# Retention attention and a gated feed-forward layer on one core: batches 0 and 1 held two positions a partition, the first stage reordered, and two groups of block 0 computed by halves of tokens

## The chip, the core and the metric

The kernel runs on one core of one Trainium2 chip. The core has five engines that each work through their own list of instructions in order and wait for each other by semaphores: TensorE (PE in the profile, its weight loads PEld), VectorE (DVE), ScalarE (ACT), GpSimd (POOL) and SyncE (SP), which here issues nearly all DMAs. Matmul results land in PSUM, which here is handed out in tiles with tags (`mm` three, `O` two, `sc` two, `st` one); GpSimd works on SBUF alone in this kernel. The metric is the device time of one execution in microseconds (us), less is better. Before: 293.27 us, the median of three runs (292.98 to 293.93).

## The reference, cut to what matters

```python
batch, n_heads, seq, head_dim = (8, 8, 576, 64)
scores = scale * np.matmul(q, k.transpose(0, 1, 3, 2))
gamma = 1.0 - 2.0 ** (-5.0 - np.arange(H))
Dmat = np.where(rel >= 0, gamma[:, None, None] ** rel[None, :, :], 0.0)   # rel = i - j
ret = scores * Dmat[None, :, :, :]
attn_out = np.matmul(ret, v)
x = attn_out.transpose(0, 2, 1, 3).reshape(B * S, H * D)      # 4608 x 512
h = x @ w_in                                                  # 512 x 2048
g = h * (1.0 / (1.0 + np.exp(-beta * h)))
out = g @ w_out                                               # 2048 x 512
```

The decay gamma^(i-j) splits into a factor of the query and one of the key's value, so `q` is multiplied by gamma^i and `v` by gamma^-j once, and the masked product needs only zeros and ones.

## The kernel before, in words

**Blocks.** The first 512 positions of each batch are one block of tokens for the feed-forward part; the last 64 positions of all eight batches form block 8. A block's feed-forward has two halves: `up` (`ph`, 16 groups of 128 columns of `w_in`, four matmuls of 512 tokens each, then Silu on ScalarE into `gT`) and `down` (`po`, or from block 3 on the seven products of `seven_mm`, chains U, W and Z). Attention of later batches is woven into the feed-forward of earlier blocks.

**Attention of batches 0 and 1.** A batch's 512 positions are four chunks of 128, one position a partition. For each chunk: `pre` casts keys to `kn` and scales values to `vn` on GpSimd; `t_k` turns `kn` on TensorE into `T`, copied to `kT`; `a_sc` makes the chunk's scores `sc`, 8 matmuls with 64 rows and 128 columns, and DVE masks them into `R`; `a_O` adds up `vn` times `R` in `O`; `a_cross` adds what comes from earlier chunks, queries times the state `sbd`; `a_st` adds the chunk to the state `st` (4 matmuls), copied to `sbd` in two halves; `a_x` copies `O` to `xT`, the transposed input of `up`. Queries are scaled by `pre_q` into `qs` (four instructions) and turned by `t_q` into `qT` in two halves of heads.

**Later batches** have their own forms (`scores`, `outputs4`, `crosses4`, `four_states`) in 64x64 tiles, four of which can be at work in four quadrants of the array; `paired` interleaves two lists of such matmuls. Their keys and queries are turned by DMA transposes on SP (`x_q`, `x_k`, line 372 in the profile).

**What sets the order.** The schedule is written out by hand. The first stage is the list of calls at the end (lines 869 to 915): each call puts its instructions into the queues of its engines, in that order. After it, `merged` walks through a list `fill` of TensorE pieces and puts the steps of several `streams` before the piece whose number they name: `d0` is the number of block 0's first down, `u1` of block 1's first up. `load_kv` and `load_q` put DMAs into SP's queue in the same way. Buffers are reused in turn (keys and values `kvn`: 6, queries `qn`: 2, `qs`: 1, `qT`: 2, `kn` and `kT`: 4, `vn`: 7, `R`: 3), and an instruction that fills one waits for the last reader of it.

**SP's queue at the start**: queries of batch 0 in two halves of heads, then keys and values chunk by chunk as `ahead` says, then `w_in` in eleven pieces and `w_out` in eight, then queries, keys and values of batch 1, and so on. Keys and values move as rows of 64 floats, 256 bytes each; queries of four positions as rows of 1,024 bytes; weights of 1,024 and 2,048 bytes.

**Warm-ups** (`warm_up`) are matmuls on zeros that stand before waits in the first stage.

## Time and profile before

| what | value |
|---|---|
| median of three runs | 293.27 us |
| profiled execution, time | 292.41 us |
| its span (first to last instruction) | 290.7 us |
| mean granted TensorE clock | 0.999 |
| TensorE busy | 281.9 us, 97% |
| VectorE, ScalarE, GpSimd busy | 186.1, 171.5, 139.1 us |
| first matmul of the first `up` starts | 18.44 us |
| first `down` of block 0 starts | 32.34 us |
| batch 1's attention on TensorE | 42.7 to 56.0 us |

The table of stretches gives the time by stage: 0 to 18.4 us is batch 0's attention, where TensorE is busy in most of each microsecond with small matmuls and warm-ups; from there to 32 us block 0's `up`; to 50 us its `down`, with batch 1's attention in its last third and in the first part of block 1's `up`; then two blocks with plain downs and, from 111 us on, the blocks with seven products; the last matmul of the last block ends at about 287 us, and the last stores end the span.

How to read the profile: a row names the line of the program, the engine, the operation, what is written from what, the shape and the number of instructions; in rows in order of time the first two numbers are start and length in us, and the brackets say how long the engine stood idle before and who ended that wait. A busy TensorE is not one at its peak, since matmuls overlap; 512 columns follow each other every 0.216 us in the `up` here, though one shows 379 ns. The profiled run is one execution, and its time lies 0.86 us under the median.

### The profile page before, as it was taken

Reading aid. Unit: us, or ns where it says so; the run is one execution under the profiler, and the core shown is the slowest. Engines: PE = TensorE matmul, PEld = TensorE weight load, DVE = VectorE, ACT = ScalarE, POOL = GpSimd, SP = SyncE. Lnnn points to the kernel's source line nnn. Section 1 sums busy time; section 2 is a strip of 40 time slices with the busy share of each in tenths; the row PEclk is TensorE's granted clock in tenths of the full one; section 3 lists DMA queues with packets and bytes.
Section 4 is the critical chain, followed back from the end, with each engine's and each line's share of the span. In section 5 each row is a group of like instructions: output and inputs, shape, how many; then the busy total and the mean of one; then the engine's idle time right before and its main releaser. Section 6 shows DMA issues by size and latency. Waiting matters only on the chain.

```text
span 290.7 us, 8297 instructions
## 1 busy us (share of the span) xinstructions
PE 281.9 (97%) x3433; PEld 175.7 (60%) x3433; DVE 186.1 (64%) x340; ACT 171.5 (59%) x301; POOL 139.1 (48%) x259
## 2 busy tenths in 40 slices
PE   8799999999999998999999999999999999999995
PEld 6554446864544554448854885578547845784584
DVE  6563555804896396279889875995597555642673
ACT  5677546686878872765158625772576156837730
POOL 4766207872499397089759539625088100000000
PEclk9999999999999999999999999999999999999999
DMA  8999999996989999988999989990779430003004
GB/s 213 218 342 386 387 283 233 240 190 123 247 180 246 253 187 201 267 225 214 183 249 265 195 231 260 189 156 2 215 176 142 92 144 3 2 28 119 0 4 143
DMA packets 128886, 54.03 MB, mean 186 GB/s; under 512 B 110400, under 2 KB 121680, under 8 KB 128848
## 3 DMA queue, kind: packets, MB, share of 16 engines
q1 hardware_dynamic: 128816, 53.49, 77.9%
q8 instruction: 27, 0.44, 0.7%
q14 instruction: 11, 0.09, 0.1%
q10 hardware_dynamic: 32, 0.01, 0.0%
HBM read 36.71 MB, written 9.44 MB: 159 GB/s over the span
## 4 chain that ended last, share of the span: by engine, by line
PE 55%; DVE 5%; POOL 4%; DMA 2%; issue 1%; ACT 0%; SPq 0%; DVEq 0%
PE ph L727 27%; PE U L764 10%; PE Z L764 7%; PE W L764 6%; DMA qn<-in_q_dram 2%; DVE sa L748 2%; PE O L509 2%; PE po L837 2%; POOL vn L305 2%; POOL kn L364 1%; PE sc L509 1%; POOL qs L323 1%; PE st L509 1%; DVE gT L732 1%; DVE R L286 1%
## 5 line engine op out<-in xcount | busy, mean ns | idle before, releaser
L727 PE MATMUL ph<-xT,w_in_sb 128*128 128x512 bf16 (+1 forms) x560 | 116.8, 364 | 0.0
L727 PEld LDWEIGHTS <-w_in_sb 128*128 128x128 bf16 x560 | 53.3, 98 | 55.2 <-POOL w_in_sb L206 0.7
L734 ACT ACTIVATE gT<-ph,beta_sb 128x512 bf16<-128x512 f32 (+1 forms) x92 | 58.4, 642 | 42.6 <-PE ph L727 41.8
L764 PEld LDWEIGHTS <-sa 128*128 128x128 bf16 x480 | 46.9, 98 | 5.8 <-issue 0.2
L732 DVE TENSOR_SCALAR gT<-hs,ratio 128x512 bf16<-128x512 f32 x48 | 25.8, 538 | 32.9 <-ACT hs L731 32.6
L364 POOL CAST kn<-kvn 128x128 bf16<-128x128 f32 (+2 forms) x80 | 35.8, 483 | 22.3 <-DMA kvn<-in_k_dram 21.8
L323 POOL TENSOR_TENSOR qs<-qn,gq 128x256 bf16<-128x256 f32 x48 | 30.5, 667 | 33.2 <-DMA qn<-in_q_dram 23.4
L748 DVE TENSOR_TENSOR sa<-gT 128x1024 bf16<-128x1024 bf16 (+1 forms) x54 | 43.9, 854 | 1.4 <-PE Z L764 1.2
L731 ACT ACTIVATE hs<-ph,beta_sb 128x512 f32<-128x512 f32 x48 | 33.0, 688 | 19.0 <-PE ph L727 18.7
L837 PE MATMUL po<-w_out_sb,gT 128*128 128x512 bf16 x192 | 43.5, 379 | 0.0
L305 POOL TENSOR_TENSOR vn<-kvn,gv 128x256 bf16<-128x256 f32 x48 | 34.3, 739 | 1.2 <-DMA kvn<-in_v_dram 0.7
L837 PEld LDWEIGHTS <-gT 128*128 128x128 bf16 x192 | 18.1, 98 | 20.6
L764 PE MATMUL U<-b,sa 128*128 128x256 bf16 x192 | 22.9, 272 | 0.1
L764 PE MATMUL Z<-b,sa 128*128 128x256 bf16 x192 | 22.9, 273 | 0.0
L286 DVE TENSOR_TENSOR R<-sc,late 128x512 bf16<-128x512 f32 x24 | 15.4, 681 | 11.4 <-issue 10.2
L764 PEld LDWEIGHTS <-gT 128*128 128x128 bf16 x192 | 18.7, 98 | 3.5
L248 DVE TENSOR_TENSOR b<-wt 128x512 bf16<-128x512 f32 x20 | 16.4, 880 | 1.9 <-ACT wt L231 1.8
L417 DVE TENSOR_TENSOR R<-sc,causal 128x512 bf16<-128x512 f32 x16 | 10.2, 686 | 4.6 <-PE sc L413 4.5
L819 PE MATMUL ph<-xT,w_in_sb 128*128 128x512 bf16 x56 | 12.4, 379 | 0.2 <-ACT xT L470 0.2
L642 ACT CAST xT<-O 128x512 bf16<-128x512 f32 x19 | 9.8, 599 | 3.5 <-PE O L509 3.5
L764 PE MATMUL W<-b,gT 128*128 128x256 bf16 x96 | 11.5, 273 | 0.0
L764 PE MATMUL U<-b,gT 128*128 128x256 bf16 x96 | 11.5, 273 | 0.0
(118 smaller groups left out, 304.8 us busy)
## 6 DMA issues: line engine op xcount, KB each, us to landing
qn<-in_q_dram SPq DMA_DIRECT2D x16, 512.0 KB, 5.8
out_dram<-ot SPq DMA_DIRECT2D x32, 256.0 KB, 3.3
kvn<-in_k_dram SPq DMA_DIRECT2D x20, 256.0 KB, 5.4
kvn<-in_v_dram SPq DMA_DIRECT2D x20, 256.0 KB, 5.1
wt<-in_moe_w_out_dram SPq DMA_DIRECT2D x8, 512.0 KB, 9.3
kvn<-in_k_dram SPq DMA_DIRECT2D x24, 128.0 KB, 4.0
kvn<-in_v_dram SPq DMA_DIRECT2D x24, 128.0 KB, 3.4
wt<-in_moe_w_in_dram SPq DMA_DIRECT2D x5, 512.0 KB, 8.2
```

What stands on the lines that cost most here:

```text
L248: nc.vector.tensor_tensor(to, x, y, op)
L286: return lambda: f(*a)
L305: nc.gpsimd.tensor_tensor(vn[:, hs], v[:, hs], g[:, hs], ALU.mult)
L323: nc.gpsimd.tensor_tensor(batch[b]["qs"][:, cs, to], q_tiles[b][:, hs, cs].rearrange("p h i d -> p i h d"), gq[:, cs, hs].unsqueeze(3).to_ ...
L364: nc.gpsimd.tensor_copy(kn[:, c % 2, to], t[:, 0, hs])
L727: nc.tensor.matmul(ph, w_in_sb[:, ko, fo * P:(fo + 1) * P], xts[m][:, ko, :, w], start=(ko == 0), stop=(ko == KO - 1))
L731: nc.scalar.activation(h, ph, ACT.Silu, scale=beta_sb[:, fo:fo + 1])
L732: nc.vector.tensor_scalar(gts[m][:, fo], h, ratio[:, fo // 2:fo // 2 + 1], None, ALU.mult)
L734: nc.scalar.activation(gts[m][:, fo, :, w], ph, ACT.Silu, scale=beta_sb[:, fo:fo + 1])
L748: nc.vector.tensor_tensor(sums_a[0][:, held_in[j], ks], quarter(m, *x, ks), quarter(m, *y, ks), op)
L764: nc.tensor.matmul(chains[c, n][:, 0 if alone else p], a, sevens[k // 2][:, j - 1, k % 2, :], start=j in (3, 4, 1) and k == 0 and (alone o ...
L837: nc.tensor.matmul(po[:, :nn], gT[:, fo, ms, :], w_out_sb[:, fo, n0:n0 + nn], start=(fo == 0), stop=(fo == FO - 1))
```

## The change

- **Loads.** Keys and values of batches 0 and 1 come in spans of 256 positions (`load_span`), two neighbouring positions a partition, so that a row is 128 floats, 512 bytes; a span's keys are one DMA of 512 KB and its values another. In SP's queue keys of the first span go before the second half of the queries.
- **Tiles.** A chunk of 128 positions is now 64 partitions times two. `pre_k` and `pre_v` take each second position (r = 0, 1); scores (`a_sc`) and outputs (`a_O`) are 64x64 tiles with 128 columns, 16 to a call, a call covering a span and half the heads (y = 0, 1); `states` is 16 matmuls of 64x64 and 64 columns for one chunk, and for the first chunk of a batch also the same with all 128 partitions, which gives the state after two chunks; `state_out` copies it. `R` is masked by a mask of 256 columns.
- **Engines.** Of batch 0, one of the four `qs` goes to GpSimd, the first `qT` copy to DVE and the second to ScalarE in two parts, one `kn` to DVE, the `beta` copy to DVE; `w_in`'s first piece is cast by GpSimd alone. Chunk 2's `O` is split in two tiles like chunk 3's.
- **Order.** The first stage is a new list. `up_spans` computes groups 0 and 1 of block 0's `up` for tokens of chunks 0 and 1 inside it, and for chunks 2 and 3 as the first piece of `fill`. In batch 1, the transpose of the second half of a span's keys moves from `d0 + 14` to `d0 + 13.4` and the scores of the first call, which need both halves, stay at `d0 + 14`; the states of chunks 0 and 1 are both at `d0 + 15`.

Cut to its core, the diff is:

```diff
...
-    ahead = [(0, 0), (0, 1), (1, 0), (1, 1), (2, 0), (3, 0), (2, 1), (3, 1)]
-    keys_first = [(0, 0), (1, 0), (0, 1), (1, 1), (2, 0), (3, 0), (2, 1), (3, 1)]
+    def load_span(b, u, j):
+
+        t = stage.tile([P, H, 2, D], F32, name="kvn", tag="kvn", bufs=NQ)
+        nc.sync.dma_start(t[:].rearrange("p h r d -> p h (r d)"),
+                          (k, v)[j][b][:, 2 * u * P:2 * (u + 1) * P].rearrange("h (p r) d -> p h (r d)", r=2))
+        span_tiles[b, u, j] = t
...
-    load_q(0)
-    for n, j in ahead:
-        load_kv(n, (j,))
+    load_q(0, (0,))
+    load_span(0, 0, 0)
+    load_q(0, (1,))
+    load_span(0, 0, 1)
+    load_span(0, 1, 0)
+    load_span(0, 1, 1)
...
-    causal = consts.tile([P, P], BF16, name="causal")
+    causal = consts.tile([P, 2, CB, PC], BF16, name="causal")
     nc.gpsimd.memset(causal[:], 1.0)
-    nc.gpsimd.affine_select(out=causal[:], in_=causal[:], pattern=[[1, CB], [CB, PC]], compare_op=ALU.is_ge,
-                            fill=0.0, base=0, channel_multiplier=-1)
+    for x in range(2):
+        w = slice(x * TL, (x + 1) * TL)
+        nc.gpsimd.affine_select(out=causal[w], in_=causal[w], pattern=[[-1, 2], [1, CB], [CB, PC]], compare_op=ALU.is_ge,
+                                fill=0.0, base=0, channel_multiplier=-2)
...
-    def cast_w_in(g, kos=None):
+    def cast_w_in(g, kos=None, alone=False):
         t = wts[g]
         f0, fn, rows = pieces[g]
         for ko in kos or range(rows[0].start, rows[-1].stop):
-            if ko % 2 == 0:
+            if ko % 2 == 0 or alone:
                 nc.gpsimd.tensor_copy(w_in_sb[:, ko, f0:f0 + fn], t[:, ko])
...
-        nc.scalar.copy(beta_sb[:], pb[:])
+        nc.vector.tensor_copy(beta_sb[:], pb[:])
...
-            e = nc.vector
+            e = nc.gpsimd if b == 0 and n == 3 else nc.vector
...
+    def pre_k(b, u, r, copy=nc.gpsimd.tensor_copy):
+
+        if (b, u) not in spans:
+            spans[b, u] = dict(kn=sb.tile([P, 2, H, D], BF16, name="kn", tag="kn", bufs=4),
+                               kT=sb.tile([P, 2, HP, P], BF16, name="kT", tag="kT", bufs=4), vn=[None] * 2, R=[None] * 2)
+            live.update({b * CB + 2 * u + x: {} for x in range(2)})
+        copy(spans[b, u]["kn"][:, r], span_tiles[b, u, 0][:, :, r])
+
+    def pre_v(b, u, r):
+
+        vn = spans[b, u]["vn"][r] = sb.tile([P, H, D], BF16, name="vn", tag="vn", bufs=7)
+        nc.gpsimd.tensor_tensor(vn[:], span_tiles[b, u, 1][:, :, r], gains(gv, 2 * u + r), ALU.mult)
...
+    def t_q(b, u, rows=(slice(0, CB),)):
+        for cs in rows:
+            T = psum.tile([P, cs.stop - cs.start, 2, P], BF16, name="T", tag="mm" if u else "O", bufs=3 if u else 2)
+            for i in range(cs.start, cs.stop):
+                for p in range(2):
+                    nc.tensor.transpose(T[:, i - cs.start, p, :], heads(batch[b]["qs"][:, i], 2 * u + p), ident[:])
+            (nc.vector.tensor_copy if u == b else nc.scalar.copy)(batch[b]["qT"][:, cs, 2 * u:2 * u + 2], T[:])
+
+    def t_k(b, u, r):
+        late_span = b and u
+        T = psum.tile([P, HP, P], BF16, name="T", tag="sc" if late_span else "O" if b or u + r == 0 else "mm",
+                      bufs=2 if b or u + r == 0 else 3)
         for p in range(HP):
-            nc.tensor.transpose(T[:, p, :], heads(live[i]["kn"], p), ident[:])
-        (nc.vector.tensor_copy if i in (CB + 2, CB + 3) else nc.scalar.copy)(live[i]["kT"], T[:])
+            nc.tensor.transpose(T[:, p, :], heads(spans[b, u]["kn"][:, r], p), ident[:])
+        (nc.vector.tensor_copy if late_span or u > r else nc.scalar.copy)(spans[b, u]["kT"][:, r], T[:])
...
+    def a_sc(b, u, y):
+        L = spans[b, u]
+        L["R"][y] = R = sb.tile([P, 2, 2, 2, P], BF16, name="R", tag="R", bufs=3)
+
+        tag = ("O" if b else "mm") if y else "sc"
+        sc = [psum.tile([P, 2, 2, P], F32, name="sc", tag=tag, bufs=3 if tag == "mm" else 2) for _ in range(2)]
+
+        def one(j, r, pp, x):
+            rhs, view = q_cols(b * CB + 2 * u + x, row_d(j), 2 * y + pp)
+            mm(view(sc[j][half(x), r, pp, :]), L["kT"][row_d(j), r, 2 * y + pp, half(x)], rhs, start=True)
+
+        paired(*[[F(one, j, r, pp, x ^ j) for r in range(2) for pp in range(2) for x in range(2)] for j in range(2)])
+        m_b = causal[:].rearrange("k r i s -> k r (i s)").unsqueeze(2).to_broadcast([P, 2, 2, P])
         for j in range(2):
             nc.vector.tensor_tensor(R[:, j], sc[j][:], m_b, ALU.mult)
...
-        return i in (CB - 1, CB + 1)
+        return i in (CB - 2, CB - 1, CB + 1)
...
+    def a_O(b, u, y, crossed=(), last=True):
+
+        L = spans[b, u]
+
+        def one(x, pp, r, hh):
+            i, p = b * CB + 2 * u + x, 2 * y + pp
+            mm(O_of(i, p)[row_d(hh)], L["vn"][r][half(x), 2 * p + hh, :], L["R"][y][half(x), hh, r, pp, :],
+               start=opens(i, p) and r == 0 and x not in crossed, stop=last and r == 1)
+
+        paired(*[[F(one, x, pp, r, hh ^ x) for pp in range(2) for r in range(2) for hh in range(2)] for x in range(2)])
...
-            nc.vector.tensor_copy(x[:, :2], view(Os[0]))
-            nc.scalar.copy(x[:, 2:], view(Os[1]))
+            (nc.vector.tensor_copy if b else nc.scalar.copy)(x[:, :2], view(Os[0]))
+            (nc.scalar.copy if b else nc.vector.tensor_copy)(x[:, 2:], view(Os[1]))
...
+    def states(b, c):
+
...
+            state_ps[b] = psum.tile([P, 2, HP, D], F32, name="st", tag="st", bufs=1)
+        st, L = state_ps[b], spans[b, c // 2]
+        for n, rows in ((0, half(0)), (1, slice(0, P))) if c == 0 else ((1, half(c % 2)),):
+            for r in range(2):
+                for p in range(HP):
+                    for j in range(2):
+                        mm(st[row_d(j), n, p, :], L["kn"][rows, r, 2 * p + j, :], L["vn"][r][rows, 2 * p + j, :],
+                           start=c == 0 and n == 0 and p == 0 and r == 0, stop=r == 1)
+
+    def state_out(b, c):
+
+        st = state_ps[b][:, min(c, 1)]
+        e = nc.vector.tensor_copy if b and c > 1 else nc.scalar.copy
         for j in range(2):
-            r, cols = slice(j * D, (j + 1) * D), slice(j * D, (j + 1) * D)
-            e = nc.vector.tensor_copy if i in (CB + 2, CB + 3) else nc.scalar.copy
             if c < CB - 1:
-                e(sbds[c][r, :, cols], st[r, :, cols])
+                e(sbds[c][row_d(j), :, row_d(j)], st[row_d(j)])
                 continue
-            e(ends[b][r, :2], st[r, :2, cols])
-            e(ends[b][(1 - j) * D:(2 - j) * D, 2:], st[r, 2:, cols])
+            e(ends[b][row_d(j), :2], st[row_d(j), :2])
+            e(ends[b][row_d(1 - j), 2:], st[row_d(j), 2:])
...
+    def up_spans(fs, u):
+
+        if u == 0:
+            gts[0] = sb.tile([P, FO, CB, P], BF16, name="gT", tag="gT", bufs=1)
+            for f in fs:
+                phs[f] = psum.tile([P, CB, P], F32, name="ph", tag="mm", bufs=3)
+        w = slice(u * 2 * PC, (u + 1) * 2 * PC)
+        for kos in (range(2), range(2, KO)):
+            for f in fs:
+                for ko in kos:
+                    nc.tensor.matmul(phs[f][:, :, w], w_in_sb[:, ko, f * P:(f + 1) * P], xts[0][:, ko, :, w],
+                                     start=u == 0 and ko == 0, stop=ko == KO - 1, skip_group_check=True)
+                    if u and ko == KO - 1:
+                        nc.scalar.activation(gts[0][:, f], phs[f][:].rearrange("f i s -> f (i s)"), ACT.Silu, scale=beta_sb[:, f:f + 1])
...
-    warm_up(5)
+    warm_up(1)
     betas()
     betas_safe()
-    for n in range(4):
+    warm_up(3)
+    for n in range(2):
         pre_q(0, n)
     t_q(0, 0)
+    for r in range(2):
+        pre_k(0, 0, r)
+        warm_up(1, 128)
+        t_k(0, 0, r)
+    for n in range(2, 4):
+        pre_q(0, n)
     warm_up(1, 128)
-    t_q(0, 1)
-    pre(0)
-    t_k(0)
+    a_sc(0, 0, 0)
+    t_q(0, 1, (slice(0, 2), slice(2, CB)))
+    for r in range(2):
+        pre_v(0, 0, r)
     warm_up(2, 128)
-    a_sc(0)
-    a_st(0)
-    pre(1)
-    t_k(1)
-    warm_up(1, 128)
-    a_cross(0, True)
-    a_O(0)
+    a_sc(0, 0, 1)
+    warm_up(2, 128)
+    states(0, 0)
+    state_out(0, 0)
+    pre_k(0, 1, 0, nc.vector.tensor_copy)
+    pre_k(0, 1, 1)
+    for c in range(2):
+        new_O(c)
+    a_O(0, 0, 0)
+    for r in range(2):
+        t_k(0, 1, r)
+    a_O(0, 0, 1, last=False)
+    a_cross(1, False)
+    state_out(0, 1)
+    for r in range(2):
+        pre_v(0, 1, r)
     a_x(0)
-    a_sc(1)
-    a_cross(1, True)
-    pre(2, (0,))
-    t_k(2)
-    a_st(1)
-    a_O(1)
-    pre(3, (0,))
-    a_sc(2)
-    t_k(3)
+    a_sc(0, 1, 0)
     a_x(1)
-    warm_up(1, 128)
-    a_sc(3)
+    a_sc(0, 1, 1)
+    warm_up(2, 128)
     a_cross(2, True)
-    pre(2, (1,))
-    a_st(2)
-    a_O(2)
+    new_O(3)
+    warm_up(2, 128)
+    states(0, 2)
+    state_out(0, 2)
+    a_O(0, 1, 0, (0,))
+    cast_w_in(0, (0, 1), True)
+    cast_w_in(0, (2, 3), True)
+    up_spans((0, 1), 0)
+    a_O(0, 1, 1, (0,))
+    a_cross(3, False)
     a_x(2)
-    pre(3, (1,))
-    warm_up(2, 128)
-    a_cross(3, True)
-    a_O(3)
-    cast_w_in(0, (0, 1))
     a_x(3)
-    cast_w_in(0, (2, 3))
-    a_st(3)
+    states(0, 3)
+    state_out(0, 3)
     cast_w_in(1)
     nc.vector.reciprocal(rbeta_sb[:], beta_sb[:])
     nc.vector.tensor_tensor(ratio[:], beta_sb[:, 0::2], rbeta_sb[:, 1::2], ALU.mult)
@@ -920,7 +966,8 @@
             nc.gpsimd.affine_select(out=m[half(x)], in_=m[half(x)], pattern=list(pattern), compare_op=ALU.is_ge, fill=0.0,
                                     base=0, channel_multiplier=-1)
 
-    fill = [F(ups, 0, (fo, fo + 1), u, tags) for fo, tags in ((0, ("mm", "mm")), (2, ("O", "O")), (4, ("sc", "sc"))) for u in range(2)]
+    fill = [F(up_spans, (0, 1), 1), lambda: None]
+    fill += [F(ups, 0, (fo, fo + 1), u, tags) for fo, tags in ((2, ("O", "O")), (4, ("sc", "sc"))) for u in range(2)]
...
     def second(i):
-        for f in (a_O, lambda j: a_cross(j, False), a_x):
+        for f in (new_O, lambda j: a_O(1, j % CB // 2, j % 2, last=False), lambda j: a_cross(j, False), a_x):
             f(i)
             f(i + 1)
-        a_st(i + 1)
+        if i == CB:
+            state_out(1, 1)
+        else:
+            states(1, 3)
+            state_out(1, 3)
...
-               [(10.3, F(load_q, 1))] + [(10.3, F(load_kv, CB + n, (j,))) for n, j in keys_first],
+               [(10.3, F(load_q, 1))] + [(10.3, F(load_span, 1, u, j)) for u in range(2) for j in range(2)],
...
-               [(d0 + 8, F(pre, 4, (0,))), (d0 + 8, F(pre, 5, (0,))), (d0 + 9, F(pre, 4, (1,))), (d0 + 9, F(pre, 5, (1,))),
-                (d0 + 12.7, F(t_k, 4)), (d0 + 14, F(t_k, 5)), (d0 + 14, F(a_sc, 4)), (d0 + 15, F(a_sc, 5)),
-                (d0 + 15, F(a_st, 4)), (d0 + 15.9, F(second, 4))],
-               [(d0 + 10, F(pre, 6, (0,))), (d0 + 10, F(pre, 7, (0,))), (d0 + 12, F(pre, 6, (1,))), (d0 + 12, F(pre, 7, (1,))),
-                (d0 + 15.95, F(t_k, 6)), (u1 + 1, F(t_k, 7)), (u1 + 2, F(a_sc, 6)), (u1 + 3, F(a_sc, 7)),
-                (u1 + 4, F(a_st, 6)), (u1 + 7, F(second, 6))]]
+               [(d0 + 8, F(pre_k, 1, 0, r)) for r in range(2)] + [(d0 + 9, F(pre_v, 1, 0, r)) for r in range(2)] +
+               [(d0 + 12.7, F(t_k, 1, 0, 0)), (d0 + 13.4, F(t_k, 1, 0, 1)), (d0 + 14, F(a_sc, 1, 0, 0)), (d0 + 15, F(a_sc, 1, 0, 1)),
+                (d0 + 15, F(states, 1, 0)), (d0 + 15, F(state_out, 1, 0)), (d0 + 15.9, F(second, 4))],
+               [(d0 + 10, F(pre_k, 1, 1, r)) for r in range(2)] + [(d0 + 12, F(pre_v, 1, 1, r)) for r in range(2)] +
+               [(d0 + 15.95, F(t_k, 1, 1, 0)), (u1 + 1, F(t_k, 1, 1, 1)), (u1 + 2, F(a_sc, 1, 1, 0)), (u1 + 3, F(a_sc, 1, 1, 1)),
+                (u1 + 4, F(states, 1, 2)), (u1 + 4, F(state_out, 1, 2)), (u1 + 7, F(second, 6))]]
...
```

More of the change, by code (lines that the diff above doesn't have):

```diff
@@ L293, in row_of @@
     def row_of(b, c):
-        return CB + 1 + c % 2 * 2 + c // 2 if b >= QB else c
+        return CB + 1 + c % 2 * 2 + c // 2
     def gains(g, c):
@@ L333, in pre @@
         if 0 not in js:
[L334 to L338 removed]
+            by_halves(live[i]["vn"], kv_tiles.pop(i)[:, 1], gains(gv, row_of(b, c)))
             return
@@ L362, in pre @@
         live[i] = dict(kn=kn[:, c % 2], kT=kT[:, c % 2], vn=vn)
-        for to, hs in turned if b >= QB else [(slice(0, H), slice(0, H))]:
+        for to, hs in turned:
             nc.gpsimd.tensor_copy(kn[:, c % 2, to], t[:, 0, hs])
@@ L401, in q_cols @@
         return batch[b]["qT"][r, :, p, cols], lambda o: o.rearrange("k (i s) -> k i s", i=CB)
-    def a_sc(i):
-        L = live[i]
-        L["R"] = R = sb.tile([P, 2, HP, P], BF16, name="R", tag="R", bufs=3)
-        tag = "mm" if i == CB - 1 else "O" if i >= E and (i - E) % 2 else "sc"
-        sc = [psum.tile([P, HP, P], F32, name="sc", tag=tag, bufs=3 if tag == "mm" else 2) for _ in range(2)]
-        for p in range(HP):
-            for j in range(2):
-                r = slice(j * D, (j + 1) * D)
-                rhs, view = q_cols(i, r, p)
-                nc.tensor.matmul(view(sc[j][:, p, :]), L["kT"][r, p, :], rhs, start=True, stop=True,
-                                 skip_group_check=True)
-        m_b = causal[:].unsqueeze(1).to_broadcast([P, HP, P])
+    def a_sc(b, u, y):
[8 more added lines that the diff above has]
+        m_b = causal[:].rearrange("k r i s -> k r (i s)").unsqueeze(2).to_broadcast([P, 2, 2, P])
         for j in range(2):
@@ L424, in new_O @@
         if split(i):
-            tags = ("sc", "sc") if i == CB - 1 else ("O", "sc")
-            live[i]["O"] = [psum.tile([P, 2, P], F32, name="O", tag=t, bufs=2) for t in tags]
+            live[i]["O"] = [psum.tile([P, 2, P], F32, name="O", tag=t, bufs=2) for t in ("O", "sc")]
         else:
```

44 lines of the change are left out of this document (5 added, 39 removed).

## The prediction

> **What bounds the kernel now.** I read the busy shares first, then busy time by microsecond, then TensorE in order of time, and last the chain that ended last. In the profile's page:
>
> ```profile
> PE 281.9 (97%) x3433; PEld 175.7 (60%) x3433; DVE 186.1 (64%) x340; ACT 171.5 (59%) x301; POOL 139.1 (48%) x259
> ```
>
> TensorE is busy 97% of the span, so a change can gain only where it is not: 290.7 - 281.9 = 8.8 us. The table of stretches puts 3.4 us of it in the first 20 us, 1.35 us in 100 to 120, and 3.4 us at the end (after the last matmul at 287.3). By microsecond (columns: PE, PEld, DVE, ACT, POOL busy, granted clock, DMA share, GB/s):
>
> ```profile
> 4.00:5.00 1.00, 1.00 (x4) 0.82 (x3) 0.54 (x3) 1.00 (x1) 0.00 (x0) 1.00 1.08 378
> 8.00:9.00 1.00, 0.40 (x5) 0.40 (x6) 0.69 (x1) 0.01 (x1) 0.87 (x2) 1.00 1.35 218
> 12.00:13.00 1.00, 0.66 (x14) 0.38 (x11) 0.70 (x2) 0.53 (x1) 0.74 (x2) 1.00 1.35 218
> 24.00:25.00 1.00, 1.00 (x6) 0.44 (x5) 0.43 (x1) 1.00 (x3) 0.56 (x2) 1.00 1.06 389
> ```
>
> Queries move in runs of 1,024 bytes at 372 GB/s on average, keys and values in runs of 256 bytes at a flat 218 GB/s from 6 to 14 us, weights at 350 to 390. The DMA queue is full in all of these rows. GpSimd waits for each key and value:
>
> ```profile
> 14.70 2.19 POOL L336 TENSOR_TENSOR vn<-kvn,gv 128x512 bf16<-128x512 f32 x2 [0.60 <-DMA kvn<-in_v_dram]
> ```
>
> and TensorE's first stage ends with the chunk that hangs on it:
>
> ```profile
> 17.20 0.40 PE L446 MATMUL O<-qT,sbd 128*128 128x128 bf16 x4
> 17.52 0.41 PE L460 MATMUL O<-R,vn 128*64 128x128 bf16 x8
> 17.87 0.40 PE L482 MATMUL st<-vn,kn 128*128 128x128 bf16 x4
> 18.44 5.34 PE L819 MATMUL ph<-xT,w_in_sb 128*128 128x512 bf16 x24 [0.17 <-ACT xT L470]
> ```
>
> From 18.44 to 100 us TensorE has next to no idle time: a microsecond saved before 18.44 is one saved at the end, and TensorE time added in batch 1 (42 to 56 us) is paid in full. The other idle place, in block 2's downs:
>
> ```profile
> 108.45 0.55 PE L509 MATMUL O<-qT,sbd 64*64 64x64 bf16 x24
> 110.03 0.19 PE L509 MATMUL st<-vn,kn 64*64 64x64 bf16 x1 [1.03 <-POOL vn L305]
> ...
> 110.61 0.38 PE L509 MATMUL st<-vn,kn 64*64 64x64 bf16 x24 [0.32 <-POOL vn L305]
> ```
>
> and the chain behind it (start, length):
>
> ```profile
> 94.68 0.58 SPq L86
> ...
> 95.31 5.49 DMA qn<-in_q_dram
> ...
> 100.86 2.44 POOL qs L323 x5
> ...
> 108.97 1.59 POOL vn L305 x2
> ```
>
> It is a relay of SP, DMA and GpSimd: a query load of batch 4 waits in SP's queue behind a key transpose, which waits for GpSimd, and so on back to the loads of batch 1.
>
> **The first stage.** TensorE's rate from 18.44 on does not change: 16 groups of `ph` take 16 x 0.864 us (24 matmuls of 512 columns in 5.2). So I ask when `up` could have started to end at the same time.
>
> *Loads.* At 16 engines 218 GB/s is 18.8 ns a run of 256 bytes, 372 is 44 ns for 1,024, and 388 is 84.5 ns for 2,048. Runs of 512 bytes are not in the trace. The straight line between 256 and 1,024 gives 27 ns (301 GB/s), that between 1,024 and 2,048 23.7 ns (345). I take 330, nearer the latter, because both its rows are on the side to which the runs grow; the ends are 218 and 372. The trace's lag from last byte to consumer is 0.95 us (first query half: 3.8 to 4.76). That lands K of span 0 at 6.3, the second query half at 7.7 (6.2 before: SP now issues it behind K), V 9.3, K of span 1 10.9, V 12.5 (before: the last V at about 15.7), and w_in starts 3.2 us earlier. The Trainium skill, "DMA: Bandwidth & Descriptors", section Specifications, calls 512 bytes the least transfer for line rate; then 372 would hold and the sum below would be 0.2 us better. No row here shows it.
>
> *Chain of engines.* With the rows' durations (GpSimd `kn` 0.61, `vn` 1.04; ACT copy 0.59; DVE `R` pair 1.29; `sbd` pair 0.76; hand-over 0.05): `kn` 6.35 to 7.70, as two casts in one queue; transpose of r=1 at 7.75; kT on ACT to 8.79; scores of y=0 at 8.84, `R` 9.29 to 10.58. Queries' second half: `qs` on DVE to 8.45 and, moved, on GpSimd to 8.87 (a 128x512 multiply, 1.04), which is over before V lands; two ACT copies, now halves, to 10.71; scores of y=1 at 10.76, `R` to 12.50. Then DVE casts `kn` of span 1, 12.41 to 12.86 (0.43, by the w_in cast of that size): this cast is moved behind two `R`s, so K landed at 10.9 waits 1.5 us, and transposes, kT on ACT (to 14.18) and `sbd` of chunk 1 (to 14.88) queue behind it. Scores of span 1 at 14.23, `R`s 14.68 to 17.17. Two `xT` copies on ACT follow `sbd`, to 15.96. States of chunk 2 at 16.19, `O` of y=0 at 16.43, the new half-token `ups` of groups 0 and 1 at 16.73 (8 matmuls of 256 columns at 0.11 = 0.88; the four w_in casts, all on GpSimd, end at 16.52), `O` of y=1 17.61, cross 17.91, `xT` to 18.73, second half of `ups` at 18.78. Of the 13.83 us of `ph`, 0.88 are then done, so this equals a start at 17.9: 0.52 us gained.
>
> The same sum over the old order gives a last `xT` at 18.28 against 18.35 in the trace. What the trace lacks is the price of 64x64 tiles with 128 columns. Those with 64 columns cost 11.7 ns each (4.5 us/384), twice that is 23.4; a set of 16 then takes 0.19 to 0.37 us, I take 0.30, since 8 of the old ones took 0.33. With 0.22 for sets and states the start is 17.6; with 0.40, 18.5. A second unknown, DVE's strided cast, costs 0.25 if it takes 0.7 (`R`'s row). So 17.3 to 19.1, short of the load case below. The edits with one answer: mask twice as wide (GpSimd idles 2.6 us there), beta copied by DVE (4.3, idle), warm-ups (cover for waits); they cost nothing while those waits last.
>
> Here a rule speaks against the change. The rows say that 64 small score matmuls took 0.58 us (100.72 to 101.30), 9 ns each. The Trainium skill, "TensorE: Matmul & The Clock Gate", section "Wait — 56ns, not 53.3ns?", says that start-to-start never falls below about 25 ns, however few columns. The trace disagrees, at 64 columns and four quadrants. By that rule a set here would take 0.40 us, and the time would be about that of the first rival, whose price is from rows.
>
> **Batch 1, 42 to 56 us.** Its order has one new wait: the transpose of r=1 now stands directly before the scores that need it, where before the scores used the other chunk. In the old rows such a transpose starts at 45.55, ACT's copy runs 45.97 to 46.56, so the scores' second half starts at 46.6 and not 46.02: 0.58 us lost, with all of block 0's downs queued behind it on TensorE. Scores win 4 x 0.03; states go from 16 matmuls (0.92 us) to 64 tiles at 15.9 ns (6.1/384), 1.02; bounds 0.8 (at the 12.5 ns of 68.03 to 68.43) and 1.8 (no overlap: 64 columns at a quarter of a 256-column matmul's 0.11); I take the row's mean, since two of four quadrants are used. Outputs: 16 in 0.30, as now. Together -0.56. `second` no longer ends on states and its cross waits for `R` no longer than before.
>
> **The stall at 110 us.** Loads of batch 1 start 3 us earlier behind weights that move earlier, and 2.1 MB at 330 instead of 218 saves 3.3 more. GpSimd's batch 1 work, which waited for DMA (12.1 us before 43.28, and more in between), ends some 6 us earlier; so do batch 2's queries (52.82 to 57.88 in the old rows), SP's transposes (58.53) and each link of the relay, unless a buffer holds it. The buffers that I followed (qn, kvn, qT, kT, vn) are free by then. GpSimd also slows in the old 78 to 94 us beside DVE's `b` (`kn` triples of 2.25 us against 0.88), and an earlier relay meets less of that. A lead of 1.35 us plus TensorE's own is enough to end the stall: +1.35, bounds 0 and 1.35. What is late next is TensorE itself.
>
> **Sum.** 0.52 - 0.56 + 1.35 = 1.3 us. The profiled run took 292.41 (span 290.7 and 1.7 around it): 291.1. The median shown, 293.27, lies 0.86 above that run, so 291.95 on its footing.
>
> **Rivals.**
> *Small tiles of 128 columns overlap only in twos.* The old score matmul shows 51 ns (3.3 us/64), so 25.6 a tile and 0.41 a set. The start is then 18.4 and gains nothing; batch 1 loses 0.58 + 0.32 (scores) + 0.44 (outputs) + 0.10 (states); stall gone +1.35: -0.1 us, 293.4. Against it the 9 ns rows; for it that 128 columns are not in them.
> *The relay is paced by something other than loads*, such as a buffer that TensorE frees. The stall stays: 293.3. For it: GpSimd idled 5.3 us before 76.39 on a wait that the trace does not name. Against: that is when a query load from 70.59 should land.
> *Slower: runs of 512 bytes move no more bytes a second than those of 256.* At 218 GB/s the start is 20.6, -2.15; batch 1 -0.56; the stall goes since TensorE comes late, +1.35: 294.6. At 250 it would be 19.4 and the sum about 0; below that the change loses. For it: 218 is as flat as a limit on bytes; against it: queries on the same queue run at 372.
> *The first stage does better*, tiles at 0.22 and loads at 360: start 17.3, 291.3.
>
> **Numbers.** About 0.3%, 0.88 us, can be told from no change. Forecast 0.42 and the better case 0.13: faster, 0.55. Small tiles 0.15 and relay 0.10: within, 0.25. Slow loads, with whatever else lengthens the first stage that much, 0.20: slower. The range 290.7 to 294.5 takes in all but the tails of the best and the last case; the forecast's own is 291.2 to 292.6.
>
> **What would show it.** GB/s of 300 or more at 6 to 12 us; first full `ups` (groups 2 and 3) near 19.7; `sc` sets near 0.3 us; an idle TensorE, ended by ACT's kT, near 45 us; no wait for `vn` near 109 us, and batch 4's query load issued at 90 us or sooner. The forecast is wrong if K and V still come at 218, if sets take 0.4 us, or if the relay holds its old times.

## The result, and the profile after

The changed kernel took 294.66 us (median of 19 runs, 293.52 to 296.26); the kernel before, on the same chip, 293.01 (19 runs), or 292.50 without three slow runs, which the ratios and medians below leave out. The ratio is 1.0069, 95% interval 1.0050 to 1.0089: slower by 0.7%. The forecast was faster, 291.95 us, with a range up to 294.5. The profiled execution took 295.33 us, its span 293.6, so 2.92 more than the profiled execution before; the medians of 294.66 and 292.50 differ by 2.16. Both kernels' executions spread over more than a microsecond, and a profile shows one of them: where a time is told below from profiles alone, the text says so.

In the page after, TensorE is busy for less time than before (281.9 then), in a longer span:

```profile
PE 280.8 (96%) x3642; PEld 178.1 (61%) x3671; DVE 181.4 (62%) x341; ACT 170.5 (58%) x300; POOL 134.4 (46%) x262
...
q8 instruction: 29, 0.48, 0.7%
```

So there is new idle time, 4 us of it. By microsecond (same columns as before) the loads do what was asked of them, though not at 330 GB/s:

```profile
8.00:9.00 1.00, 1.00 (x19) 0.87 (x16) 0.52 (x2) 0.81 (x2) 0.36 (x1) 1.00 1.18 305
11.00:12.00 1.00, 0.82 (x20) 0.76 (x20) 0.33 (x2) 0.20 (x1) 1.00 (x2) 1.00 1.20 290
```

TensorE in order of time, end of the first stage and first full group (`L839`, forecast near 19.7 us):

```profile
17.09 0.23 PE L529 MATMUL st<-vn,kn 64*64 64x64 bf16 x4
17.15 0.29 PE L529 MATMUL O<-R,vn 64*64 64x128 bf16 x6
18.15 0.31 PE L529 MATMUL O<-R,vn 64*64 64x128 bf16 x8 [0.71 <-issue]
18.39 1.05 PE L854 MATMUL ph<-xT,w_in_sb 128*128 128x256 bf16 x8
...
21.33 3.62 PE L839 MATMUL ph<-xT,w_in_sb 128*128 128x512 bf16 x15
```

In the middle of one call's 16 tiles TensorE stands still, from the last start at 17.22 to the next at 18.15, with no releaser ("issue"). I call such an idle time a stop. The tiles after it need nothing that those before did not have. The same happens twice later, in code that the change did not touch:

```profile
82.00 0.23 PE L529 MATMUL O<-qT,sbd 64*64 64x64 bf16 x6
82.96 0.23 PE L529 MATMUL O<-qT,sbd 64*64 64x64 bf16 x5 [0.72 <-issue]
```

```profile
104.51 0.32 PE L529 MATMUL st<-vn,kn 64*64 64x64 bf16 x17
105.50 0.32 PE L529 MATMUL st<-vn,kn 64*64 64x64 bf16 x15 [0.66 <-issue]
```

(The 0.16 us before some `po` rows after a set are no such waits: there the record of the first matmul is missing, as 29 records are in all.) In batch 1 the forecast's new wait is there:

```profile
46.94 0.31 PE L529 MATMUL sc<-qT,kT 64*64 64x128 bf16 x8
47.68 0.31 PE L529 MATMUL sc<-qT,kT 64*64 64x128 bf16 x8 [0.44 <-ACT kT L416]
...
55.33 0.44 PE L529 MATMUL st<-vn,kn 64*64 64x64 bf16 x16
55.70 1.48 PE L747 MATMUL ph<-xT,w_in_sb 128*128 128x256 bf16 x12
```

The last two rows are a set of states; in the kernel before the same place was

```profile
53.07 0.39 PE L482 MATMUL st<-vn,kn 128*128 128x128 bf16 x4
53.29 1.47 PE L727 MATMUL ph<-xT,w_in_sb 128*128 128x256 bf16 x12
```

In block 2's downs the wait for `vn` is gone, with SP's load of batch 4's queries at 90.40 instead of 94.68:

```profile
112.42 0.43 PE L529 MATMUL O<-qT,sbd 64*64 64x64 bf16 x24
112.72 0.19 PE L529 MATMUL st<-vn,kn 64*64 64x64 bf16 x1
```

Last, the end. The last output's DMA is put in 2.1 us later than before and lands 2.9 us later. The DMA view of 290.4 to 292.8 us (GB/s in 40 slices) shows a transfer of the instruction queue ahead of the last output's packets, and single packets at the end:

```profile
GB/s 358 358 239 137 290 0 0 0 0 0 0 222 273 307 358 341 290 171 86 17 0 17 0 17 0 17 17 0 17 0 34 0 0 0 0 0 0 0 0 0
...
q8 instruction: 1, 0.02, 2.4%
```

The last output's 128 packets start 0.65 us after its issue, as before. That 16 KB packet runs from 290.66 to 291.60, and the last eight packets of the output follow it one by one, to 292.3, as if they had waited behind it on one DMA engine. From the end of SP's issue to SP's wait ending, the last output took 2.40 us here, 1.58 in the kernel before. The last packet lands 1.9 us after the issue here and 1.2 us in each of the other thirteen profiles, none of which has an instruction transfer at this place.

I followed the lag behind the kernel before by the starts of the 106 `gT` activations, which both kernels have in the same order. Of the span's 2.92 us: first stage +1.08, batch 1 +1.59, the stop at 82 us +0.54, that at 105 +0.66, the `vn` wait -1.68, small changes -0.10, the last output +0.82.

### The profile page after: what moved, and what is told of

It is laid out like the page before. It is cut to its first block, busy times and chain, and to the rows that moved or that the text cites. A ratio compares the mean times of both kernels' runs of the same rounds, so it can differ in the third digit from the quotient of the medians.

```text
span 293.6 us, 8739 instructions
## 1 busy us (share of the span) xinstructions
PE 280.8 (96%) x3642; PEld 178.1 (61%) x3671; DVE 181.4 (62%) x341; ACT 170.5 (58%) x300; POOL 134.4 (46%) x262
## 4 chain that ended last, share of the span: by engine, by line
PE 90%; DVE 3%; DMA 2%; issue 2%; ACT 1%; POOL 1%; SPq 0%; DVEq 0%; POOLq 0%
PE ph L747 37%; PE po L872 14%; PE U L784 11%; PE W L784 7%; PE Z L784 7%; PE O L529 4%; PE ph L839 3%; DMA qn<-in_q_dram 2%; PE sc L529 2%; PE st L529 2%; DVE sum L565 1%; DVE sbd L293 1%; PE O L466 1%; POOL qs L333 1%; PE T L407 0%
## 5 line engine op out<-in xcount | busy, mean ns | idle before, releaser
L747 PE MATMUL ph<-xT,w_in_sb 128*128 128x512 bf16 (+1 forms) x542 | 114.3, 363 | 1.8 <-issue 0.6
L752 DVE TENSOR_SCALAR gT<-hs,ratio 128x512 bf16<-128x512 f32 x48 | 25.1, 525 | 34.3 <-ACT hs L751 33.8
L768 DVE TENSOR_TENSOR sa<-gT 128x1024 bf16<-128x1024 bf16 (+1 forms) x54 | 44.7, 868 | 0.7 <-PE Z L784 0.4
L330 POOL TENSOR_TENSOR qs<-qn,gq 128x256 bf16<-128x256 f32 x48 | 31.7, 692 | 27.3 <-DMA qn<-in_q_dram 20.6
L872 PE MATMUL po<-w_out_sb,gT 128*128 128x512 bf16 x183 | 42.0, 379 | 1.1 <-issue 0.9
L312 POOL TENSOR_TENSOR vn<-kvn,gv 128x256 bf16<-128x256 f32 x48 | 31.5, 679 | 9.8 <-issue 8.9
L367 POOL CAST kn<-kvn 128x128 bf16<-128x128 f32 (+1 forms) x72 | 25.7, 396 | 17.9 <-DMA kvn<-in_k_dram 17.9
L255 DVE TENSOR_TENSOR b<-wt 128x512 bf16<-128x512 f32 x20 | 13.5, 736 | 3.2 <-ACT wt L238 1.8
L784 PE MATMUL W<-b,sa 128*128 128x256 bf16 x96 | 11.5, 273 | 0.0
```

Source lines behind the costliest of these rows:

```text
L312: nc.gpsimd.tensor_tensor(vn[:, hs], v[:, hs], g[:, hs], ALU.mult)
L330: nc.gpsimd.tensor_tensor(batch[b]["qs"][:, cs, to], q_tiles[b][:, hs, cs].rearrange("p h i d -> p i h d"), gq[:, cs, hs].unsqueeze(3).to_ ...
L367: nc.gpsimd.tensor_copy(kn[:, c % 2, to], t[:, 0, hs])
L747: nc.tensor.matmul(ph, w_in_sb[:, ko, fo * P:(fo + 1) * P], xts[m][:, ko, :, w], start=(ko == 0), stop=(ko == KO - 1))
L752: nc.vector.tensor_scalar(gts[m][:, fo], h, ratio[:, fo // 2:fo // 2 + 1], None, ALU.mult)
L768: nc.vector.tensor_tensor(sums_a[0][:, held_in[j], ks], quarter(m, *x, ks), quarter(m, *y, ks), op)
```

## The experiments

**Theory 1**: TensorE runs out of instructions. The instruction queue moves 16 KB at a time, 29 times for 7,338 TensorE records (27 for 6,892 before; a record is a matmul or a weight load in the trace), so about 256 instructions a block. The three stops lie at records 450, 1,978 and 2,487: 1,528 and 509 apart, six and two blocks less some missing records. A 64x64 tile takes two instructions and 64 of them start within 0.53 us (111.89 to 112.42), so a block is soon used up: the 256 records before each of the three stops took 4.4 to 4.6 us. The next block's transfer started 2.7 to 2.8 us after the first of these 256, at 15.59, 80.11 and 102.78 us, and TensorE went on 2.56, 2.85 and 2.72 us later. **Theory 2**: those sets wait for data or buffers that the trace does not name.

The Trainium skill, "Runtime: NRT & Kernel Launch", section "Instruction fetch mechanics", has the blocks of 16 KiB and 256 instructions, fetched by a DMA queue of the sequencer's own while the present block runs, and calls the cost of crossing into the next one mostly hidden. The counts agree; the 0.7 us stops, and the 2.18 us below, do not.

**e1: 36 instructions more ahead of the work.** Twenty tiny matmuls (40 instructions) replace a warm-up (4).

```diff
+    def pad(n):
+        ph = psum.tile([P, MB], F32, name="ph", tag="mm", bufs=3)
+        for _ in range(n):
+            nc.tensor.matmul(ph[:TL, :TL], ident[:TL, :TL], ident[:TL, :TL], start=True, stop=True, skip_group_check=True)
...
-    warm_up(3)
+    warm_up(2)
+    pad(20)
```

> The changed kernel with one 256-column warm-up matmul fewer and 20 matmuls of a 64x64 tile on the identity in its place before the first query transposes: 36 instructions more in TensorE's stream, the work otherwise unchanged. Theory 1 (TensorE runs out of instructions: the profile's instruction queue moves 16 KB for each 256 of them, and in a dense run of small tiles 256 are used up before the next block is there): all block borders move 36 instructions earlier in the work; the idle time without releaser in the middle of the sets at 17.4 (0.71 us), 82.2 (0.72) and 104.8 (0.66) goes, and the 16 KB transfer beside the last output (0.82 us) too; the time falls by 1.9 to 2.9 us against the changed kernel, to a ratio of 0.997 to 1.000 against the kernel before. Theory 2 (these sets wait for data or for a buffer that the trace does not name): the three idle times stay where they are, and the time stays at a ratio of 1.007.

**e2: batch 1's first key transposes a piece earlier.**

```diff
-               [(d0 + 12.7, F(t_k, 1, 0, 0)), (d0 + 13.4, F(t_k, 1, 0, 1)), (d0 + 14, F(a_sc, 1, 0, 0)),
+               [(d0 + 11.7, F(t_k, 1, 0, 0)), (d0 + 12.7, F(t_k, 1, 0, 1)), (d0 + 14, F(a_sc, 1, 0, 0)),
```

> The changed kernel with batch 1's first two key transposes one piece of the first down group earlier, so that a piece of 0.86 us stands between the second one and the score set that reads its copy. Theory 1 (batch 1's loss is, for the first part, the 0.44 us in which TensorE waits for ScalarE's kT with nothing left to issue): the wait at 47.2 goes, batch 1 loses about 1.1 us instead of 1.6 against the kernel before, the time falls by 0.4 to 0.6 us, if the borders of the instruction blocks do not move (they stay: the number of instructions is the same). Theory 2 (ScalarE is the limit there and only another wait takes its place): the time stays within 0.2 us of the changed kernel.

**e3: the kernel before with the same 36 instructions.**

```diff
-    warm_up(5)
+    warm_up(4)
     betas()
     betas_safe()
+    pad(20)
```

> The kernel before with the same 36 instructions more ahead of its work. Theory 1 (instruction blocks of 256): the kernel before has no idle time without releaser now; with its borders 36 instructions earlier, two of them come to lie about both ends of one dense set near 189 us, and TensorE stands idle there for 1.5 to 3.5 us with no releaser, so that the kernel before becomes slower by about as much: ratio 1.005 to 1.012. Theory 2 (the idle times of the changed kernel come from its data): nothing moves, ratio 0.999 to 1.001.

**e4: e1 and e2 together.**

> Both edits to the changed kernel at once: 36 instructions more, and batch 1's first key transposes a piece earlier. Theory 1 on both counts: the gains add up, 2.3 to 3.5 us below the changed kernel, ratio 0.995 to 0.999 against the kernel before. If the idle times come from data: the gain of the key transposes alone, ratio 1.005.

| kernel | median us | ratio to before, 95% interval | profiled, us |
|---|---|---|---|
| e1 | 294.85 | 1.0067 (1.0039 to 1.0094) | 295.32 |
| e2 | 294.27 | 1.0066 (1.0036 to 1.0096) | 292.99 |
| e3 | 296.54 | 1.0139 (1.0083 to 1.0196) | 295.34 |
| e4 | 293.68 | 1.0018 (0.9991 to 1.0045) | 294.59 |

(Each group of runs has a chip of its own, with the kernel before beside it: compare the ratios.) e3 decides between the theories. The kernel before, whose profile had no stop at all, got one where its borders were moved to, and lost 1.4%. In the profiles the stop is 2.3 of the 2.94 us between the two spans:

```profile
189.40 0.32 PE L514 MATMUL O<-qT,sbd 64*64 64x64 bf16 x16
191.96 0.19 PE L514 MATMUL O<-qT,sbd 64*64 64x64 bf16 x1 [2.18 <-issue]
```

In e1 the stops at 82 and 105 are gone, and that of the first stage has moved to other work, states instead of outputs. It is record 450 again:

```profile
18.10 0.28 PE L534 MATMUL st<-vn,kn 64*64 64x64 bf16 x6
18.60 0.28 PE L534 MATMUL st<-vn,kn 64*64 64x64 bf16 x6 [0.22 <-issue]
```

But e1 was no faster. The key transposes behind its pad took 0.63 us instead of 0.39, though the granted clock reads 1.00 there, and the first stage ended 0.71 us later. Why is open: behind the same pad in e3 they took 0.40, and in e7 and e9, which have no pad, the first ones took 0.63 too. And what it had gained by 160 us was lost near 170, where VectorE's additions `sa` were slow and TensorE waited for them. The first row is e1's, the second e2's, whose additions met no work of GpSimd:

```profile
165.73 6.21 DVE L773 TENSOR_TENSOR sa<-gT 128x1024 bf16<-128x1024 bf16 x6
```

```profile
164.57 3.69 DVE L768 TENSOR_TENSOR sa<-gT 128x1024 bf16<-128x1024 bf16 x6
```

GpSimd multiplies the last batch's queries from 165.58 to 173.00 in e1 and from 169.36 on in e2. One addition takes 1.10 us beside it and 0.68 without. The Trainium skill, "SBUF — State Buffer", section "SBUF: two separate sides", says that VectorE and GpSimd share one pair of ports, and that a VectorE instruction with two inputs in SBUF and a GpSimd instruction that reads SBUF hold it in turn, each for its whole length. The rows agree in that the additions get longer; they do not show who held what.

e2's mechanism is there too: the two half sets have become one, with no wait, and batch 1 loses 0.63 us less.

```profile
46.67 0.42 PE L529 MATMUL sc<-qT,kT 64*64 64x128 bf16 x16
47.02 1.04 PE L872 MATMUL po<-w_out_sb,gT 128*128 128x512 bf16 x4
```

All seven profiles with this edit show it between 0.63 and 0.64. In the times neither e1 nor e2 alone is told from the changed kernel; both together are.

**e5: a pad of the whole array.** The four 256-column warm-ups become 30 bf16 matmuls of the whole array; 44 instructions more.

```diff
+    warm_b = consts.tile([P, P], BF16, name="warm_b")
+    nc.vector.memset(warm_b[:], 0.0)
...
+            nc.tensor.matmul(ph[:, :P], warm_b[:], warm_b[:], start=True, stop=True, skip_group_check=True)
...
-    warm_up(1)
+    pad(8)
     betas()
     betas_safe()
-    warm_up(3)
+    pad(22)
```

> The first pad ran on one quarter of TensorE's array, and the transposes and warm-ups after it took 0.63 and 0.74 us where the changed kernel's take 0.39 and 0.44, 0.7 us in all; so it measured two things. Here the four 256-column f32 warm-ups are 30 bf16 ones of the whole array: 44 instructions more in the same time. Theory 1 (blocks of 256 instructions): no cost ahead of the first scores; the idle times without releaser at 82 and 105 us gone, the one of the first stage gone or under 0.3 us, first down group at 32.4 to 32.8 us instead of 33.4; last output's landing 1.6 us after its issue instead of 2.4; 292.6 to 293.4 us, unless VectorE's sa additions meet GpSimd's query products near 165 us as in the first pad's run, which would give 0.9 to 1.2 of it back. Theory 2 (the first stage is late by its loads and GpSimd's casts, and the idle time only stands in their place): first down group at 33.2 us or later although the idle time is gone.

**e6: e5 with e2's edit.**

> The same, and batch 1's first key transposes a piece earlier, which took 0.63 us out of batch 1 in its own run: 0.6 us below the run with the 30 warm-ups alone, 292.0 to 292.8 us, ratio 0.995 to 0.999. If the gains before 150 us are taken back near 165 us by VectorE and GpSimd, both this and the run without the key edit end within 0.3 us of each other.

**e7: without the half groups.**

```diff
-    up_spans((0, 1), 0)
...
-    fill = [F(up_spans, (0, 1), 1), lambda: None]
-    fill += [F(ups, 0, (fo, fo + 1), u, tags) for fo, tags in ((2, ("O", "O")), (4, ("sc", "sc"))) for u in range(2)]
+    fill = [F(ups, 0, (fo, fo + 1), u, tags) for fo, tags in ((0, ("mm", "mm")), (2, ("O", "O")), (4, ("sc", "sc"))) for u in range(2)]
```

> The changed kernel without up_spans: block 0's first two up groups as full ones behind the first stage, as before. Theory 1 (the half groups fill the wait for xT between the last O sets and the first full group, and no more): first down group 0.1 to 0.5 us later than the changed kernel's 33.41. Theory 2 (they only move 0.9 us of the same work forward past sets that would have been ready): first down group within 0.1 us or earlier. 16 instructions fewer ahead of batch 1, so the borders of the blocks lie 16 instructions later in the work: the idle time of the first stage stays (0.5 to 0.9 us), those at 82 and 105 us may grow or shrink by some tenths.

**e8: span loads in runs of 256 bytes.**

```diff
...
+        src = (k, v)[j][b][:, 2 * u * P:2 * (u + 1) * P].rearrange("h (p r) d -> p h r d", r=2)
+        for r in range(2):
+            nc.sync.dma_start(t[:, :, r], src[:, :, r])
```

> The changed kernel with each span load as two transfers of 256-byte runs, as the loads of the kernel before. Theory 1 (the length of the runs sets the rate of these loads): 218 GB/s over 6 to 14 us where the changed kernel moves 290 to 330, the last V span there about 3 us later, GpSimd's vn, its casts of w_in and the first up groups later by as much, first down group at 35.5 to 36.5 us, the time 2 to 3 us up. Theory 2 (the load rate is set by something else): within 0.5 us of the changed kernel.

| kernel | median us | ratio to before, 95% interval | stop in the first stage | first down group |
|---|---|---|---|---|
| changed | 294.66 | 1.0069 (1.0050 to 1.0089) | 0.71 | 33.41 |
| e5 | 293.77 | 1.0060 (1.0026 to 1.0095) | 1.35 | 33.92 |
| e6 | 292.81 | 0.9993 (0.9962 to 1.0024) | 0.69 | 33.12 |
| e7 | 293.68 | 1.0021 (0.9987 to 1.0056) | none named | 33.20 |
| e8 | 295.71 | 1.0073 (1.0035 to 1.0112) | none | 34.00 |

The stops at 82 and 105 are absent from all seven profiles with a pad and present, one or both, in the five of the changed form without one (changed, e2, e7, e8, e9), though in e7 and e9 the one that is left is of 0.18 us. The stop of the first stage did not go, and e5's pad did not keep the transposes fast either (0.63 and 0.57 us). In e5 the stop is the longest of the first stage in any run:

```profile
16.76 0.22 PE L536 MATMUL st<-vn,kn 64*64 64x64 bf16 x2
18.33 0.34 PE L536 MATMUL st<-vn,kn 64*64 64x64 bf16 x10 [1.35 <-issue]
```

Over the nine profiles that have it, TensorE goes on with record 450 at 17.5 to 18.6 us, 2.3 to 2.7 us after the block's transfer starts at 15 to 16.3, however early it used up the block before. The kernel before reaches record 450 at 34 us, among full groups. The changed first stage has about half as many instructions again (303 records by 18.44 before, 450 by 17.2 now), and the block sets its end: from record 450 to the first down it is 15.27 us in both the changed kernel and e2, 15.53 in e1 and e4, and 15.60 in e5 and e6, pairs with the same first stage.

e8 shows what that does to the gain of the loads. Its rate fell to 218 GB/s and GpSimd's last `vn` came 1.65 us later, but its half groups started no later than those of the changed kernel, 18.20 against 18.39:

```profile
12.00:13.00 1.00, 1.00 (x24) 0.84 (x26) 0.96 (x2) 0.00 (x0) 0.46 (x1) 1.00 1.33 218
```

```profile
17.85 0.41 PE L530 MATMUL O<-R,vn 64*64 64x128 bf16 x13
18.20 1.42 PE L855 MATMUL ph<-xT,w_in_sb 128*128 128x256 bf16 x8
```

The 2 to 3 us of the expectation were 0.17 at the first full group and 0.58 at the first down, where TensorE also waited for a cast of `w_in` at 25.35. The long runs buy almost nothing there, because the changed kernel waits for its block instead. e8 does not: its block's transfer started at 13.15, 0.2 us after TensorE came to record 194, one block ahead of 450, and in the changed kernel 2.8 us after it, when 1,024-byte rows of `w_in` already moved. Why the transfer starts late there, no run shows.

e8 also brought SP's load of batch 4's queries back to 95.74 us (90.40 in the changed kernel): the relay's lead is that of the loads. But the wait for `vn` did not come back with it. GpSimd's `vn` pair ended at 110.25 (110.56 in the kernel before, 108.28 in the changed), and TensorE itself was so late, at the set at 113.39, that it found it ready.

e7 has the outcome of theory 2: without the half groups the first down is 0.21 us earlier, 0.13 of it because record 450 came at 18.02 instead of 18.15 (between two starts TensorE stood 0.31 us there, though no stop is named).

**e9, e10, e11, e12: for a kernel that beats both.** e9 is e2 and e7 together; e10 adds e5's warm-ups; e11 adds to that a later load of the last batch's queries; e12 adds to e11 that all four `qs` of batch 0 are VectorE's.

```diff
-            st += [(at - 30, F(load_q, b))]
+            st += [(at - (25.9 if b == B - 1 else 30), F(load_q, b))]
...
-            e = nc.gpsimd if b == 0 and n == 3 else nc.vector
+            e = nc.vector
```

> The changed kernel with batch 1's key transposes a piece earlier and without the half up groups, with the warm-ups as they were. If the two gains add up (0.6 us out of batch 1 and, from the run without the half groups, 0.95 us at the end of the profile): 292.9 to 293.3 us. TensorE's instruction borders lie where they lay in the run without half groups, so an idle time without releaser near 105 us may be back, 0.2 to 0.9 us, in some executions.

> The same with the 30 bf16 warm-ups (44 instructions more). Theory 1 (blocks of 256 instructions): no idle time without releaser behind the first stage, and a narrower spread of the times; 292.2 to 292.8 us. In the first stage the border lies in front of the last states and O sets, where the block is not there before 17.7 to 18.3 us, whatever the work ahead of it: an idle time of 0.5 to 1.3 us, and the first down group no earlier than 32.9 us.

> The same, with the last batch's query load put behind its four key and value tiles' loads in SP's queue, so that it is issued 5 to 8 us later. Theory 1 (VectorE's bf16 additions sa take 1.10 us beside GpSimd's query products and 0.68 alone, and TensorE waits for them near 167 and 171 us when the products start at 163 to 166 us): the products start at 169 us or later, the six additions take 0.68 us each, the two waits of 0.43 us go, 0.9 to 1.2 us below the run before it: 291.2 to 291.8 us, ratio 0.992 to 0.997 against the kernel before. Theory 2 (the additions are slow for another reason): no change, or slower where the last batch's queries come late.

> The run before it, with the last piece of batch 0's query product back on VectorE (0.69 us a piece there, 1.48 on GpSimd in these profiles). Theory 1 (the first stage without idle times for instructions is still 0.5 us behind the kernel before because this piece on GpSimd holds the second query transposes and with them the second score set): the second half of T q starts at 9.8 to 10.0 us instead of 10.3 to 10.7, the second score set 0.3 to 0.5 us earlier, first down group at 32.5 to 32.8 us where no idle time for instructions falls into the first stage; 0.3 to 0.5 us below the run before. Theory 2 (V's landings and GpSimd's products of V and casts of w_in set the first stage): the scores come earlier, the first down group does not.

| kernel | median us | ratio to before, 95% interval | stop in the first stage | first down group |
|---|---|---|---|---|
| e9 | 293.21 | 1.0037 (1.0014 to 1.0060) | 0.58 | 33.06 |
| e10 | 293.26 | 1.0039 (1.0013 to 1.0065) | 1.08 | 33.50 |
| e11 | 293.00 | 1.0032 (1.0011 to 1.0052) | none named | 32.88 |
| e12 | 293.14 | 1.0017 (0.9993 to 1.0042) | 1.07 | 33.63 |

None beats the kernel before; e4, e6, e7 and e12 are not told from it, e6 although its additions took 1.10 us. e10 came out as forecast in its stops, but its times did not spread less (292.3 to 295.2). e9's time did (292.9 to 293.3 was said), but its stops lie at 81.57 (0.18) and, not forecast, at 135.71 (0.41, record 3,507, 2.73 us after a transfer), not at 105. One execution of e11, at 1,624 us, is left out. e11's edit worked, the products start at 173.18 and the additions take 0.68, but e10's profile had no collision either, so its 0.25 us is no proof of the price. e12 has the outcome of theory 2, but not its mechanism. The second query transposes no longer wait for GpSimd, and the states start at 12.03 (12.32 in e11, but 11.76 in e10, so that a gain is not shown). What sets the end is the block: from record 450 to the first down it is 15.81 us in e10, e11 and e12 alike, and e11 is the earliest of them because its block was there at 17.07.

```profile
12.03 0.86 PE L536 MATMUL st<-vn,kn 64*64 64x64 bf16 x32
...
16.54 0.22 PE L536 MATMUL st<-vn,kn 64*64 64x64 bf16 x2
17.83 0.34 PE L536 MATMUL st<-vn,kn 64*64 64x64 bf16 x10 [1.07 <-issue]
```

## Why the prediction was wrong

*First stage, forecast 0.52 gained, 1.08 lost.* The step that failed is "States of chunk 2 at 16.19, `O` of y=0 at 16.43, the new half-token `ups` of groups 0 and 1 at 16.73". It priced tiles by their own time and took their instructions as given; the three came at 16.88, 17.07 and 18.39, and between the last two lies the stop at 17.2 us, which no step had. It is up to 0.92 of the 1.60 us. Even without it the stage would have lost some 0.16, not gained. The rest is sizes, read from the rows and not tested one by one. Loads went at 288 to 306 GB/s from 8 to 13 us, the lower of the two line fits, not 330: V of span 1 was used at 13.97 instead of 12.5. `qs` on GpSimd took 1.48 us, not 1.04. The score sets were right: 0.29 and 0.35 us against 0.30.

*Batch 1, forecast 0.56 lost, 1.59 lost.* The wait for kT was right in place and nearly in size (0.44 idle for 0.58), and e2 took it out. The states were mis-sized, and that is the second step that failed: "64 tiles at 15.9 ns (6.1/384), 1.02". A set of 16 takes 0.37 us from its start to the next matmul's (55.33 to 55.70), where four 128x128 matmuls took 0.22 (53.07 to 53.29). The three sets (32, 16 and 16 tiles) cost 1.47 us, not 1.02, against 0.90 before, so 23 ns a tile. Why these short sets cost more than those of 384 is open. A wait of 0.18 us for VectorE's `xT`, which "its cross waits for `R` no longer than before" left out, is part of the rest.

*The `vn` stall, forecast 1.35 gained, 1.68 gained.* The relay came earlier as forecast, and nearly to its mark: the query load at 90.40 us (at 90 or sooner, it was said), and e8 ties that lead to the loads. That the stall went is in part luck. TensorE came 3.9 us later than before by then, from its losses, which alone is more than the stall (the rival of slow loads had said so), and in e8 it was gone without the lead.

*What no term held*: 0.54 and 0.66 us at 82 and 105 us, and 0.82 us at the last output, all from where the instruction borders fall. With the stop of the first stage that is 2.94 us of the profile, as much as the whole loss in that execution. In the times the share is not settled: e1 and e5, which take away two of the stops, were each slower elsewhere.

*Rivals.* Small tiles in twos: refuted for the scores by sets of 0.25 to 0.35 us (one of 0.50, at 53.40, stands where the old one took 0.46). A relay not paced by loads: refuted by e8. Runs of 512 bytes as slow as 256: refuted as a mechanism (about 300 against 218 GB/s); that its 294.6 us is nearly the measured time is chance. The stops came from a mechanism that no rival named.

## What to carry to other kernels

Count instructions as well as time: where matmuls are cut into smaller tiles, see how many microseconds TensorE takes for 256 of them, and what fills the DMA queues then; here 4.4 to 5.5 us were too few in the first stage of nine profiles, and 4.9 enough in e8, where the transfer started at once. Here an idle time "issue" of over 0.2 us in the middle of a set was such a border, and a few dummy instructions ahead of everything move it, to a better place or a worse one. A gain ahead of a late resource is lost there, whatever its size.

## What the runs showed of the hardware that was not expected

- The same 36 matmul instructions, which compute nothing, cost the kernel before 1.4% (e3).
- At all sixteen stops of over 0.2 us TensorE went on 2.3 to 3.1 us after the start of a 16 KB instruction transfer.
- With a 16 KB instruction transfer beside the last output's packets, the end came 0.82 us later (one profile).
- VectorE's bf16 addition of 128x1024 takes 1.10 us beside GpSimd's multiplies and 0.68 alone.
- The same key transposes took 0.39 us (changed kernel) or 0.63 (e1), with the granted clock read as 1.00 in both.
